# Last Z and Y staged whole in bf16, four PSUM tags from the third output unit, late units and output rows spread anew

## The chip, the cores and the metric

The kernel runs on one core of one Trainium2 chip. The metric is device time in microseconds (us), the median of several executions. A profile of one execution gives what each engine did: TensorE (PE, with PEld for its weight loads), VectorE (DVE), ScalarE (ACT), GpSimd (POOL) and SyncE (SP, which issues output DMAs here).

## The reference

Two layers follow each other. The first is a linear attention with feature maps; its result, with heads put side by side, is the input of the second, a mixing of the lowest 64 Fourier modes along the sequence, with a residual and a dense layer.

```python
batch, n_heads, seq, head_dim = (8, 8, 576, 64); d_feat = 128; d_model = 512; n_modes = 64
def phi(x):
    proj = np.einsum('bhsd,df->bhsf', x, w_phi)
    proj = proj - np.max(np.abs(proj), axis=-1, keepdims=True)
    return np.concatenate([np.exp(proj), np.exp(-proj)], axis=-1)
q_p, k_p = (phi(q), phi(k))
kv = np.einsum('bhsf,bhsd->bhfd', k_p, v)
num = np.einsum('bhsf,bhfd->bhsd', q_p, kv)
den = np.einsum('bhsf,bhf->bhs', q_p, np.sum(k_p, axis=2))[..., None] + 1e-06
x = (num / den).transpose(0, 2, 1, 3).reshape(B, S, H * D)

X = np.fft.rfft(x, axis=1)[:, :n_modes]            # Xr, Xi
Yr = einsum('bmd,mde->bme', Xr, w_r) - einsum('bmd,mde->bme', Xi, w_i)
Yi = einsum('bmd,mde->bme', Xr, w_i) + einsum('bmd,mde->bme', Xi, w_r)
y = np.fft.irfft(Yr + 1j * Yi, n=S, axis=1)        # other modes are zero
u = x + y
out = (u + np.maximum(u @ w_ch, 0.0)).astype(np.float32)   # (8, 576, 512)
```

## The kernel before, in words

A sequence of 576 positions is five chunks, c = 0 to 4: chunks 0 to 3 hold 128 positions each, chunk 4 holds 64. The attention runs over 32 steps, and its result stays in SBUF as `xs_all`, in bf16, one slot of 128 partitions x 512 per (batch b, chunk c), at index 5b + c. Beside it, the forward transform (`x_mm`) fills `XT`, and the mode products begin: 32 groups of weights (`weights`, DMAs on GpSimd's queue, three buffers) are multiplied in `mode_mm` and summed in `mode_sum`. The first 22 groups lie inside the attention's steps, the last ten in a loop behind it. GpSimd scales v in the attention (`vscale`, L270 and L275), VectorE divides (L335, L336).

`u @ w_ch` is split. x @ w_ch is made early, chunk by chunk, as `xw` (`flip_x`, `times_w`). The rest is the inverse transform of Y @ w_ch, called Z. So every output chunk is, with `CI` the inverse transform's matrix:

- psB = xw + CI * Z, then relu (ScalarE, L780) into the output tile;
- psA = x + CI * Y, then added to the output tile (VectorE, L793).

**Z and Y by batch.** The last eight groups of weights (gi = 0 to 7) give complete rows of Y; a pair of them, P = gi // 2, gives 32 rows (modes and parts) for all 8 batches. `by_batch` (L691) multiplies them by w_ch into `psZ` (PSUM tag T0) and by the identity into `psR` (tag T1). Both have 128 partitions: batch j + 4h lies in partitions 32j to 32j + 31, half h. The tiles `zall` and `yall`, which the inverse transform reads, want those rows in partitions 32P to 32P + 31 for each batch. So `copy` moves a quarter, 32 partitions x 2 x 512, at a time: Z by ScalarE (L712), Y by VectorE (L713). These calls are put in the list `copies` and taken from it one by one between other work. For the last pair, P = 3, there are five calls: the first half of Z and Y and batch 0; the second half and batch 4; then batches 1 and 5, 2 and 6, 3 and 7. One is made before the first output unit and one behind each of the units 0 to 3.

**Output units.** There are 20 units n: 16 whole units of two chunks (128 x 2 x 512), and four half units that pair chunk 4 of batches b and b + 4 (units 4, 9, 14 and 15). Units 0 to 4 are batches 0 and 4, 5 to 9 batches 1 and 5, 10 to 14 batches 2 and 6, 15 to 19 batches 3 and 7. For each, in this order of issue: `add_xw` (L771), `add_z` (L778 and the relu L780), `spec` (L787 x, L790 Y, and the add L793). psB and psA of a unit take PSUM tags T2 and T3, or T0 and T1:

```python
u["tags"] = ("T2", "T3") if n % 2 == 0 or n < 4 else ("T0", "T1")
```

A PSUM tag has one buffer, so a unit's first matmul into psA waits until VectorE's add has read the unit before it in that tag, and psB waits for the relu.

**Late units.** In ten whole units TensorE leaves x out of psA, and GpSimd adds it to the output tile afterwards (L797). For these, x is brought to output order earlier, by a permuting matmul and a ScalarE copy back into `xs_all` (`reordered`, L686 and L688), one or two at a time behind some groups of weights. `late` names them: units 2, 3, 5, 7, 8, 10, 12, 13, 16 and 17.

**Output DMAs.** SyncE issues them in program order, two per unit (256 KB each; 128 KB for a half unit): those of a late unit two units later (`LAG`), the others behind their own unit. Every engine works in program order; the order written here is kept as it is (`manual_schedule`).

Of the kernel before, what the change touches and what calls it, by code (L numbers as in the profile page):

```python
# [12 lines left out]
BF16 = mybir.dt.bfloat16  # L13
# [5 lines left out]
B_, H_, S_, D_ = 8, 8, 576, 64  # L19
NMODES = 64  # L20
DMODEL = 512
NCH = 5
# [4 lines left out]
def kernel(  # L27
# [11 lines left out]
    nc = tc.nc  # L39
# [116 lines left out]
    def weights(k):  # L156
        g, gi = groups[k]
        wt = {}
        for ri, w in ((0, moe_w_r), (1, moe_w_i)):
            t = pw.tile([128, 8, DMODEL], BF16, name=f"w{'ri'[ri]}", tag=f"w{ri}")  # L160
            if gi >= 0:
                nc.gpsimd.dma_start(  # L162
                    t, w[8 * gi:8 * gi + 8, g * 128:(g + 1) * 128, :].rearrange("m p e -> p m e"))
            else:
                for x in range(2):
                    mx = 16 * (-1 - gi) + 8 * x
                    nc.gpsimd.dma_start(
                        t[64 * x:64 * x + 64],
                        w[mx:mx + 8, g * 64:(g + 1) * 64, :].rearrange("m p e -> p m e"))
            wt[ri] = t  # L170
        W[k] = wt
# [252 lines left out]
    def mode_sum(k, psY, pb=None):  # L424
        g, gi = groups[k]
        if gi < 0:
            G = -1 - gi
            if g == 0:
                nc.vector.tensor_copy(Yacc[:, 2 * G:2 * G + 2, :], psY)
            else:  # L430
                nc.vector.tensor_tensor(
                    out=Yacc[:, 2 * G:2 * G + 2, :], in0=psY, in1=Yacc[:, 2 * G:2 * G + 2, :],
                    op=ALU.add)
        elif g < 3:
            nc.vector.tensor_tensor(  # L435
                out=Yacc[:, gi, :], in0=psY, in1=Yacc[:, gi, :], op=ALU.add)
        else:
            yst = pb.tile([128, DMODEL], BF16, name="yst", tag="yst", bufs=2)
            nc.vector.tensor_tensor(out=yst, in0=psY, in1=Yacc[:, gi, :], op=ALU.add)
            return yst  # L440
# [187 lines left out]
    pb = ctx.enter_context(tc.tile_pool(name="pb", bufs=2))  # L628
# [6 lines left out]
    yall = pb.tile([128, B_, DMODEL], BF16, name="yall", bufs=1)  # L635
    zall = pb.tile([128, B_, DMODEL], BF16, name="zall", bufs=1)
# [3 lines left out]
    todo = list(range(N_EARLY, B_ * NCH, 2))  # L640
    ahead = []
    copies = []
# [11 lines left out]
    def times_w():  # L654
        i, sT = ahead.pop(0)
        ps = psum.tile([128, 2, DMODEL], F32, name="psW", tag="T2")
        for x in range(2):
            for dc in range(4):
                nc.tensor.matmul(ps[:, x, :], lhsT=sT[:, x, dc, :], rhs=wchb[:, dc, :],  # L659
                                 start=(dc == 0), stop=(dc == 3))  # L660
        nc.scalar.copy(xw[:, i - N_EARLY:i + 2 - N_EARLY, :], ps)  # L661

    def pieces(n):
        for _ in range(n):
# [7 lines left out]
                copies.pop(0)()  # L672


    late = {0: ((1, 0), (1, 2)), 1: ((0, 0), (1, 0), (1, 2)), 2: ((0, 0), (1, 0), (1, 2)),
            3: ((0, 0), (0, 2))}
    reorder = sorted((b + 4 * x) * NCH + c for b in range(4) for x, c in late[b])

    def reordered(tag):
        i = reorder[0]  # L680
# [10 lines left out]
    def by_batch(sY, P):  # L691
        cols = [sY[:, dc].rearrange("p g c -> p (g c)") for dc in range(4)]
        psZ = psum.tile([128, 2, DMODEL], F32, name="psZ", tag="T0")
        psR = psum.tile([128, 2, DMODEL], F32, name="psR", tag="T1")

        def mm_z(h):
            for dc in range(4):
                for j in range(4):
                    nc.tensor.matmul(psZ[32 * j:32 * j + 32, h, :], lhsT=cols[dc][:, j + 4 * h::8],
                                     rhs=wchb[:, dc, :], start=(dc == 0), stop=(dc == 3))  # L700

        def mm_r(h):
            for dc in range(4):
                for j in range(4):
                    nc.tensor.matmul(
                        psR[32 * j:32 * j + 32, h, dc * 128:(dc + 1) * 128],
                        lhsT=cols[dc][:, j + 4 * h::8], rhs=ident_b, start=True, stop=True)

        def copy(j, h=None, one=False):
            r = slice(32 * j, 32 * j + 32)  # L710
            bs, hs = (slice(j, None, 4), slice(0, 2)) if h is None else (j + 4 * h, h)
            nc.scalar.copy(zall[32 * P:32 * P + 32, bs, :], psZ[r, hs, :])  # L712
            (nc.scalar.copy if one else nc.vector.tensor_copy)(  # L713
                yall[32 * P:32 * P + 32, bs, :], psR[r, hs, :])

        if P < 3:
            for f in (mm_z, mm_r):
                for h in range(2):
                    f(h)
            copies.extend([lambda j=j: copy(j) for j in range(4)])  # L720
        else:

            copies.extend([lambda: (mm_z(0), mm_r(0), copy(0, 0)),
                           lambda: (mm_z(1), mm_r(1), copy(0, 1)),
                           lambda: copy(1), lambda: copy(2), lambda: copy(3, None, True)])

    with tc.manual_schedule():
        plan = {22: 3, 23: 3, 24: 2, 25: 2, 26: 2, 27: 1, 28: 2, 29: 1, 30: 1, 31: 0}
        while k_out < 32:
            k = k_out  # L730
            gi = groups[k][1]
            while k_in < min(k_out + NW, 32):
                weights(k_in)
                k_in += 1
            yst = mode_sum(k, mode_mm(k, "T3"), pb)
            k_out += 1
            if yst is not None:
                if ahead:
                    times_w()
                pt = psum.tile([128, 4, 128], BF16, name="ptY", tag="T3")  # L740
                for dc in range(4):
                    nc.tensor.transpose(pt[:, dc, :], yst[:, dc * 128:(dc + 1) * 128], ident_b)
                if gi % 2 == 0:
                    sY = pb.tile([128, 4, 2, 128], BF16, name="sY", tag="sY")
                nc.vector.tensor_copy(sY[:, :, gi % 2, :], pt)
                if gi % 2 == 1:
                    by_batch(sY, gi // 2)
            pieces(plan[k])
            if k <= 24 or k % 2 == 0:
                assert not copies  # L750
                for tag in ("T0", "T1"):
                    if reorder:
                        reordered(tag)
            if k == 30:
                times_w()
        assert not todo and not ahead and not reorder and len(copies) == 5

# [39 lines left out]
    units = []  # L799
    for b in range(4):  # L800
        of = [pw.tile([128, 4, DMODEL], F32, name="of", tag=f"w{x}") for x in range(2)]
        o4 = Yacc[:, 2 * b, :]
        us = []
        for x in range(2):
            out_v = out[b + 4 * x].rearrange("(p n) e -> p n e", n=9)
            for c in (0, 2):
                us.append(dict(bc=((b + 4 * x, c), (b + 4 * x, c + 1)), o=of[x][:, c:c + 2, :],
                               late=(x, c) in late[b], half=False,
                               dmas=[(out_v[:, 5 * jj + c:5 * jj + c + 2, :],
                                      of[x][jj::2, c:c + 2, :]) for jj in range(2)]))  # L810
        u4 = dict(bc=((b, 4), (b + 4, 4)), o=o4, late=False, half=True,
                  dmas=[(out[b + 4 * x].rearrange("(p n) e -> p n e", n=9)[:, 4, :],
                         o4[64 * x:64 * x + 64]) for x in range(2)])
        units += [u4] + us if b == 3 else us + [u4]

    with tc.manual_schedule():
        LAG = 2
        copies.pop(0)()
        for n in range(len(units) + LAG):
            if n < len(units):  # L820
                u = units[n]
                u["tags"] = ("T2", "T3") if n % 2 == 0 or n < 4 else ("T0", "T1")
                add_xw(u)
                add_z(u)
                spec(u)
                if copies:
                    copies.pop(0)()
            for lag, is_late in ((LAG, True), (0, False)):
                if 0 <= n - lag < len(units) and units[n - lag]["late"] == is_late:
                    for dst, src in units[n - lag]["dmas"]:  # L830
                        nc.sync.dma_start(dst, src)

# [29 lines left out]
```

## Time and profile before

| what | us |
|---|---|
| median of 3 runs (460.96 to 462.92) | 460.98 |
| the profiled execution's own time | 459.81 |
| its span, first to last instruction | 458.02 |
| last weights land (wi of group 31) | 413.01 |
| last Z starts (L699) | 415.67 |
| last add on VectorE (L793) ends | 452.00 |
| last output DMA lands | 456.75 |
| busy in the span: PE / DVE / ACT / POOL | 302.9 / 299.2 / 263.7 / 195.2 |

Times in the views are counted from the start of the span. A row of a group gives its line, engine, operation, output and inputs with shapes, count, then busy time, the mean ns of one, and the idle time before them with what ended it. A row of a timeline gives start and duration. A row of the chain of waits gives the piece of work that the next piece waited for; "issue" is time in which nothing shown was waited for. The clock granted to TensorE is 1.00 of full speed in every stretch from 380 to 452.

### The profile page before, as it was taken

How to read it: one execution, taken by the hardware profiler on the slowest of the kernel's cores; microseconds unless marked ns; L12 is line 12 of the kernel's file. 1: busy time of each engine (PE TensorE's matmuls, PEld its weight loads, DVE VectorE, ACT ScalarE, POOL GpSimd, SP SyncE). 2: the span in 40 equal slices, each digit the busy share in tenths (PEclk: the TensorE clock that was granted, in tenths of full speed). 3: DMA queues.
4: the chain of work that ended last, by engine and by line, in shares of the span. 5: the costliest groups of instructions: out<-in, count | busy, mean ns of one | idle time of the engine just before them, and what ended most of it. 6: DMA issues, size and time to landing. Idle time of an engine off the chain costs nothing.

```text
span 458.0 us, 11074 instructions
## 1 busy us (share of the span) xinstructions
PE 302.9 (66%) x4637; PEld 196.9 (43%) x4637; DVE 299.2 (65%) x418; ACT 263.7 (58%) x531; POOL 195.2 (43%) x246
## 2 busy tenths in 40 slices
PE   3465687755587677646464665676678878867893
PEld 2354465543454545534343443343344544433341
DVE  6588889867988788866656473766332274464774
ACT  4575787843676868755545453755333445663762
POOL 4956567445563346634344332533021113000593
PEclk9987999975976979997769685988999999999998
DMA  6999999999999999999999999999999999991488
GB/s 181 193 230 216 213 210 218 229 207 229 218 218 218 229 218 229 219 228 217 219 207 221 216 219 218 207 209 206 207 207 207 207 207 207 207 173 50 170 317 292
DMA packets 84385, 97.31 MB, mean 212 GB/s; under 512 B 3312, under 2 KB 77168, under 8 KB 84336
## 3 DMA queue, kind: packets, MB, share of 16 engines
q0 software_dynamic: 75600, 76.49, 100.6%
q1 hardware_dynamic: 8576, 20.06, 12.6%
q8 instruction: 36, 0.59, 0.5%
q14 instruction: 13, 0.11, 0.1%
q10 hardware_dynamic: 160, 0.07, 0.1%
HBM read 163.64 MB, written 9.44 MB: 378 GB/s over the span
## 4 chain that ended last, share of the span: by engine, by line
DMA 30%; DVE 23%; issue 21%; PE 10%; POOL 7%; ACT 7%; SPq 1%; DVEq 0%; ACTq 0%; POOLq 0%
DMA wi<-in_moe_w_i_dram 19%; DVE mkq L233 7%; DMA wr<-in_moe_w_r_dram 7%; DMA q<-in_q_dram 4%; DVE xs_all L336 4%; DVE nd L322 3%; DVE tB L315 3%; ACT AA L240 3%; POOL vaug L270 2%; ACT e L262 2%; DVE of L793 2%; PE psNB L305 2%; PE psB L771 1%; PE psB L778 1%; PE psA L790 1%
## 5 line engine op out<-in xcount | busy, mean ns | idle before, releaser
L270 POOL TENSOR_TENSOR vaug<-vn,ee 128x576 bf16<-128x576 f32 x64 | 72.7, 1156 | 59.5 <-ACT ee L255 53.6
L240 ACT ACTIVATE AA<-psT 128x1024 bf16<-128x1024 f32 x64 | 62.0, 1021 | 42.3 <-PE psT L208 41.8
L162 POOL DMA_DIRECT2D wr<-in_moe_w_r_dram x24 | 21.9, 911 | 115.9 <-PE psY L416 109.5
L262 ACT ACTIVATE e<-mkq 64x4 f32<-64x4 f32 (+1 forms) x128 | 26.3, 206 | 66.3 <-DVE mkq L233 64.0
L244 ACT ACTIVATE AA<-psk 128x1024 bf16<-128x1024 f32 x64 | 61.3, 1009 | 0.0
L416 PE MATMUL psY<-wi,XT 128*32 128x512 bf16 x192 | 24.1, 448 | 29.1 <-DMA wi<-in_moe_w_i_dram 29.1
L416 PEld LDWEIGHTS <-XT 128*32 128x32 bf16 x384 | 17.7, 167 | 55.9 <-issue 47.9
L233 DVE TENSOR_REDUCE mkq<-psk 128x8 f32<-128x1024 f32 x32 | 38.8, 1212 | 0.8 <-PE psk L199 0.7
L233 DVE TENSOR_REDUCE mkq<-psq 128x8 f32<-128x1024 f32 x32 | 38.9, 1217 | 0.3
L435 DVE TENSOR_TENSOR Yacc<-psY,Yacc 128x512 f32<-128x512 f32 x16 | 11.0, 689 | 42.6 <-PE psY L416 42.5
L797 POOL TENSOR_TENSOR of<-of,xs_all 128x1024 f32<-128x1024 f32 x10 | 21.1, 2130 | 41.5 <-DVE of L793 41.5
L661 ACT CAST xw<-psW 128x1024 bf16<-128x1024 f32 x17 | 17.2, 1012 | 36.5 <-PE psW L659 36.5
L286 PE MATMUL kvz<-vaug,AA 64*128 64x65 bf16 x1152 | 29.5, 211 | 9.7 <-POOL vaug L275 8.0
L190 DVE COPY kT<-ptr 128x640 bf16<-128x640 bf16 x32 | 15.7, 491 | 30.5 <-PE ptr L184 30.5
L416 PE MATMUL psY<-wr,XT 128*32 128x512 bf16 x192 | 24.2, 458 | 16.0 <-DMA wr<-in_moe_w_r_dram 7.3
L315 DVE TENSOR_TENSOR tB<-psNB,e 128x650 f32<-128x650 f32 x32 | 26.6, 833 | 11.4 <-PE psNB L305 10.8
L659 PE MATMUL psW<-wchb,sT 128*128 128x512 bf16 x136 | 32.2, 379 | 2.1 <-ACT xw L661 2.1
L336 DVE TENSOR_TENSOR xs_all<-nd,rden 128x640 bf16<-128x640 f32 x32 | 31.6, 988 | 1.1
L305 PEld LDWEIGHTS <-AA 128*128 128x128 bf16 x640 | 28.4, 108 | 8.9 <-issue 8.5
L286 PEld LDWEIGHTS <-AA 64*128 64x128 bf16 x1152 | 25.3, 107 | 14.5 <-issue 10.4
L208 PE MATMUL psT<-qT,w 64*128 64x512 bf16 x64 | 14.6, 446 | 23.5 <-DVE mkq L233 23.3
L322 DVE TENSOR_TENSOR nd<-psNA,tB 128x650 f32<-128x650 f32 x32 | 26.7, 835 | 4.1 <-DVE tB L315 0.5
(130 smaller groups left out, 707.3 us busy)
## 6 DMA issues: line engine op xcount, KB each, us to landing
wr<-in_moe_w_r_dram POOLq DMA_DIRECT2D x24, 1024.0 KB, 24.3
wi<-in_moe_w_i_dram POOLq DMA_DIRECT2D x24, 1024.0 KB, 28.4
wr<-in_moe_w_r_dram POOLq DMA_DIRECT2D x16, 512.0 KB, 14.9
wi<-in_moe_w_i_dram POOLq DMA_DIRECT2D x16, 512.0 KB, 18.6
out_dram<-of SPq DMA_DIRECT2D x32, 256.0 KB, 2.4
vn<-in_v_dram SPq DMA_DIRECT2D x24, 288.0 KB, 5.7
q<-in_q_dram POOLq DMA_DIRECT2D x12, 288.0 KB, 19.5
k<-in_k_dram POOLq DMA_DIRECT2D x12, 288.0 KB, 19.3
```

The source lines that it names most:

```text
L233: nc.vector.tensor_reduce(out=o, in_=i, axis=AX.X, op=ALU.max, apply_absolute_value=True)
L240: nc.scalar.activation(AA[:, 0, ab, 0:1024].rearrange("f (x j p) -> f j x p", j=2, p=64), st["psT"].rearrange("f j (x p) -> f j x p", p=64 ...
L244: nc.scalar.activation(AA[:, 1, ab, 0:1024].rearrange("p (c j f) -> p j c f", c=4, j=2), st["psk"], ACT.Exp, scale=sc)
L262: nc.scalar.activation(e2[64 * jj:64 * jj + 64, hh, 0:NCH - jj], mkq[64 * hh:64 * hh + 64, 1, 5 * jj:5 + 4 * jj], ACT.Exp, scale=2.0)
L270: nc.gpsimd.tensor_tensor(out=vaug[:, ab, :, 0:64], in0=st["v"], in1=ee[:, ab, :].unsqueeze(2).to_broadcast([128, 9, D_]), op=ALU.mult,)
L286: nc.tensor.matmul(kvz[:, hh, ab * 65:(ab + 1) * 65], lhsT=AA[r, 1, ab, 128 * j:128 * j + 128], rhs=vaug[r, ab, j, :], start=(j == 0), sto ...
L305: nc.tensor.matmul(p[:, hh, 65 * c:65 * c + 65], lhsT=AA[:, 0, ab, x:x + 128], rhs=kvzF[:, hh, ab * 65:(ab + 1) * 65], start=True, stop=True,)
L315: nc.vector.tensor_tensor(out=tB, in0=st["psNB"], in1=e2.unsqueeze(3).to_broadcast([128, 2, NCH, 65]), op=ALU.mult,)
L322: nc.vector.tensor_tensor(out=nd, in0=st["psNA"], in1=st["tB"], op=ALU.add)
L336: nc.vector.tensor_tensor(out=xo, in0=nd[:, :, :, 0:64], in1=rden.to_broadcast([128, 2, NCH, 64]), op=ALU.mult,)
L416: nc.tensor.matmul(psY[32 * j:32 * j + 32, :], lhsT=XT[:, c0:c0 + 32, m], rhs=wt[ri][:, 2 * j + par, :], start=(par == 0 and ri == 0), sto ...
L659: nc.tensor.matmul(ps[:, x, :], lhsT=sT[:, x, dc, :], rhs=wchb[:, dc, :], start=(dc == 0), stop=(dc == 3))
```

## The change

For P = 3, each half of Z and Y is still made by TensorE as before, and batch 0's rows are copied from PSUM as before (`first`). Behind the second half (`rest`), ScalarE copies all of psZ, 128 x 1024, into a new bf16 tile `stz` in SBUF, and VectorE all of psR into `sty`. The rows of the other batches then move from these tiles into `zall` and `yall`, from SBUF to SBUF: batch 4 by VectorE at once (two copies of 32 x 512), batches 1 and 5 by GpSimd (two copies of 32 x 1024), batches 2 and 6 by VectorE behind unit 5, and 3 and 7 by VectorE behind unit 8 (two copies of 32 x 1024 each). ScalarE has no further copies.

Tags T0 and T1 are used from unit 3 on, and all four alternate from there.

Ten units are late as before, with unit 18 in place of unit 17. The order in which x is brought to output order is that of the index, so index 35 follows where 17 stood in between; behind weight group 24 there is one such copy instead of two, and behind group 30 two instead of one.

For batches 1, 2, 5 and 6 (units 5 to 8 and 10 to 13) the rows of chunks 0 to 3 go out together, in two DMAs of 512 KB per batch, behind the second of the two units (one unit later, or three where it is late). Other late units' DMAs come three units later instead of two. 32 output DMAs replace 40.

```diff
@@ -672,9 +672,8 @@
                 copies.pop(0)()
 
 
-    late = {0: ((1, 0), (1, 2)), 1: ((0, 0), (1, 0), (1, 2)), 2: ((0, 0), (1, 0), (1, 2)),
-            3: ((0, 0), (0, 2))}
-    reorder = sorted((b + 4 * x) * NCH + c for b in range(4) for x, c in late[b])
+    late = {(b, 0) for b in range(1, B_)} | {(4, 2), (5, 2), (6, 2)}
+    reorder = sorted(b * NCH + c for b, c in late)
 
     def reordered(tag):
         i = reorder[0]
@@ -706,23 +705,46 @@
                         psR[32 * j:32 * j + 32, h, dc * 128:(dc + 1) * 128],
                         lhsT=cols[dc][:, j + 4 * h::8], rhs=ident_b, start=True, stop=True)
 
-        def copy(j, h=None, one=False):
+        rows = slice(32 * P, 32 * P + 32)
+
+        def copy(j):
             r = slice(32 * j, 32 * j + 32)
-            bs, hs = (slice(j, None, 4), slice(0, 2)) if h is None else (j + 4 * h, h)
-            nc.scalar.copy(zall[32 * P:32 * P + 32, bs, :], psZ[r, hs, :])
-            (nc.scalar.copy if one else nc.vector.tensor_copy)(
-                yall[32 * P:32 * P + 32, bs, :], psR[r, hs, :])
+            nc.scalar.copy(zall[rows, j::4, :], psZ[r])
+            nc.vector.tensor_copy(yall[rows, j::4, :], psR[r])
 
         if P < 3:
             for f in (mm_z, mm_r):
                 for h in range(2):
                     f(h)
             copies.extend([lambda j=j: copy(j) for j in range(4)])
-        else:
-
-            copies.extend([lambda: (mm_z(0), mm_r(0), copy(0, 0)),
-                           lambda: (mm_z(1), mm_r(1), copy(0, 1)),
-                           lambda: copy(1), lambda: copy(2), lambda: copy(3, None, True)])
+            return
+
+
+
+        st = {}
+
+        def first():
+            mm_z(0)
+            mm_r(0)
+            nc.scalar.copy(zall[rows, 0, :], psZ[0:32, 0, :])
+            nc.vector.tensor_copy(yall[rows, 0, :], psR[0:32, 0, :])
+
+        def rest():
+            mm_z(1)
+            mm_r(1)
+            for nm, ps, f in (("z", psZ, nc.scalar.copy), ("y", psR, nc.vector.tensor_copy)):
+                st[nm] = pb.tile([128, 2, DMODEL], BF16, name=f"st{nm}", bufs=1)
+                f(st[nm], ps)
+            nc.vector.tensor_copy(zall[rows, 4, :], st["z"][0:32, 1, :])
+            nc.vector.tensor_copy(yall[rows, 4, :], st["y"][0:32, 1, :])
+            move(1, nc.gpsimd)
+
+        def move(j, eng):
+            r = slice(32 * j, 32 * j + 32)
+            eng.tensor_copy(zall[rows, j::4, :], st["z"][r])
+            eng.tensor_copy(yall[rows, j::4, :], st["y"][r])
+
+        copies.extend([first, rest, lambda: move(2, nc.vector), lambda: move(3, nc.vector)])
 
     with tc.manual_schedule():
         plan = {22: 3, 23: 3, 24: 2, 25: 2, 26: 2, 27: 1, 28: 2, 29: 1, 30: 1, 31: 0}
@@ -753,7 +775,7 @@
                         reordered(tag)
             if k == 30:
                 times_w()
-        assert not todo and not ahead and not reorder and len(copies) == 5
+        assert not todo and not ahead and not reorder and len(copies) == 4
 
 
 
@@ -801,32 +823,35 @@
         of = [pw.tile([128, 4, DMODEL], F32, name="of", tag=f"w{x}") for x in range(2)]
         o4 = Yacc[:, 2 * b, :]
         us = []
+        whole = b in (1, 2)
         for x in range(2):
             out_v = out[b + 4 * x].rearrange("(p n) e -> p n e", n=9)
             for c in (0, 2):
+                c0 = 0 if whole else c
+                is_late = (b + 4 * x, c) in late
                 us.append(dict(bc=((b + 4 * x, c), (b + 4 * x, c + 1)), o=of[x][:, c:c + 2, :],
-                               late=(x, c) in late[b], half=False,
-                               dmas=[(out_v[:, 5 * jj + c:5 * jj + c + 2, :],
-                                      of[x][jj::2, c:c + 2, :]) for jj in range(2)]))
-        u4 = dict(bc=((b, 4), (b + 4, 4)), o=o4, late=False, half=True,
+                               late=is_late, half=False, lag=3 if is_late else 1 if whole else 0,
+                               dmas=[(out_v[:, 5 * jj + c0:5 * jj + c + 2, :],
+                                      of[x][jj::2, c0:c + 2, :]) for jj in range(2)]
+                               if c == 2 or not whole else []))
+        u4 = dict(bc=((b, 4), (b + 4, 4)), o=o4, late=False, half=True, lag=0,
                   dmas=[(out[b + 4 * x].rearrange("(p n) e -> p n e", n=9)[:, 4, :],
                          o4[64 * x:64 * x + 64]) for x in range(2)])
         units += [u4] + us if b == 3 else us + [u4]
 
     with tc.manual_schedule():
-        LAG = 2
         copies.pop(0)()
-        for n in range(len(units) + LAG):
+        for n in range(len(units) + 3):
             if n < len(units):
                 u = units[n]
-                u["tags"] = ("T2", "T3") if n % 2 == 0 or n < 4 else ("T0", "T1")
+                u["tags"] = ("T2", "T3") if n % 2 == 0 or n < 2 else ("T0", "T1")
                 add_xw(u)
                 add_z(u)
                 spec(u)
-                if copies:
+                if n in (0, 5, 8):
                     copies.pop(0)()
-            for lag, is_late in ((LAG, True), (0, False)):
-                if 0 <= n - lag < len(units) and units[n - lag]["late"] == is_late:
+            for lag in (3, 1, 0):
+                if 0 <= n - lag < len(units) and units[n - lag]["lag"] == lag:
                     for dst, src in units[n - lag]["dmas"]:
                         nc.sync.dma_start(dst, src)
 
```

## The prediction

> **What bounds the kernel now.** I read the busy time by stretches first, for where each engine stands at the end of the run; then the chain of waits behind that stretch; then the groups by form, for durations; then the timeline of two places much earlier, where VectorE and GpSimd meet. The windows view (columns: PE, PEld, DVE, ACT, POOL busy, granted clock, DMA share, GB/s):
>
> ```profile
> core 0: us, PE busy (x) PEld busy (x) DVE busy (x) ACT busy (x) POOL busy (x), PEclk, DMA share, GB/s
> ...
> 413.00:417.00 4.00, 2.63 (x49) 1.69 (x49) 1.12 (x2) 0.18 (x1) 0.00 (x0) 1.00 0.02 4
> ...
> 421.00:429.00 8.00, 5.26 (x25) 1.80 (x23) 6.18 (x6) 7.57 (x8) 2.58 (x2) 1.00 0.33 132
> 429.00:437.00 8.00, 7.91 (x41) 3.33 (x40) 5.85 (x6) 4.67 (x6) 5.27 (x3) 1.00 0.74 270
> ```
>
> Until 413 the weights' DMA sets the pace. From 421 to 429 ScalarE is full (7.57 of 8 us) and TensorE is not; from 429 on TensorE is (7.91). The chain of waits says the same:
>
> ```profile
> 388.44 24.57 DMA wi<-in_moe_w_i_dram
> ...
> 422.21 1.24 DVE of L793
> ...
> 424.13 0.56 DVE yall L713
> 424.69 0.03 issue
> 424.72 1.24 DVE of L793
> ```
>
> The last weight lands at 413.01; nothing in the change makes it land sooner. In 421 to 428 the chain goes through VectorE's adds (L793) and the copies of Y between them (L713): units 0 to 4 share one PSUM pair (T2, T3), and each waits for the one before.
>
> ```profile
> L797 POOL TENSOR_TENSOR of<-of,xs_all 128x1024 f32<-128x1024 f32 x10 | 21.1, 2130 | 41.5 <-DVE of L793 41.5
> L793 DVE TENSOR_TENSOR of<-psA,of 128x1024 f32<-128x1024 f32 x16 | 19.6, 1224 | 7.9 <-ACT of L780 7.4
> ...
> L712 ACT CAST zall<-psZ 32x1024 bf16<-32x1024 f32 x3 | 3.0, 1002 | 0.1
> ...
> L713 DVE CAST yall<-psR 32x1024 bf16<-32x1024 f32 x2 | 2.4, 1222 | 0.1
> ```
>
> A copy of 32 rows out of PSUM costs ScalarE 1.00 and VectorE 1.22 us, as much as one of 128 rows (L661, 1.01 for 128x1024). That is what staging whole saves. The price is on another row: the new copies are VectorE copies from SBUF to SBUF in bf16 while GpSimd works. The kernel before has one such copy (L507):
>
> ```profile
> 107.33 2.43 DVE L507 COPY ident_p<-ident_b 128x128 bf16<-128x128 bf16 x1
> 107.39 2.27 POOL L270 TENSOR_TENSOR vaug<-vn,ee 128x576 bf16<-128x576 f32 x2
> ```
>
> A 128-column copy took 2.43 us and ended 0.10 us after two GpSimd operations did. Casts of 576 columns that met no GpSimd operation (L154) took 0.40 and 0.45. The same again with an operation of two SBUF inputs:
>
> ```profile
> 118.65 2.29 POOL L270 TENSOR_TENSOR vaug<-vn,ee 128x576 bf16<-128x576 f32 x2
> 118.66 0.22 DVE L335 RECIPROCAL rden<-nd 128x10 f32<-128x10 f32 x1
> 118.91 2.72 DVE L336 TENSOR_TENSOR xs_all<-nd,rden 128x640 bf16<-128x640 f32 x1
> ```
>
> L336 has a median of 825 ns; here 2.72, as at 33.63 (3.29). GpSimd's second operation went ahead of the waiting VectorE each time, three times with L507.
>
> **Part by part.** I laid the rows end to end from 415.67, where the last Z starts, engine by engine in program order: 0.43 us for a pair of 512-column matmuls (0.215 in a half unit), the relu 0.63 after the Z matmuls start, 1.02 for the relu (0.60), 1.23 for the add (0.68), 2.12 for GpSimd's add, 0.64 for each output DMA's issue, 2.37 from issue to landing, 1.3 from the last landing to the end of the span. The order of before gives a last add at 451.89 and a span of 457.98, measured 452.00 and 458.02. So the rules hold to 0.1 us, and differences below are against 457.98. That execution took 459.81 against a median of 460.98, 0.25% apart; I add the difference to the median.
>
> *Spread of late units.* Index 35 takes the place of 17, so the reordering copies of x shift: two instead of one after weight group 30. The second waits for the copies of Y that end at 410.51; then 0.43, a psW of 1.72, and the first four of group 31's matmuls can start at 412.8. The wi landing at 413.01 hides that with 0.04 us left; a late arrival would cost up to 0.3. I take 0.
>
> *Copies.* ScalarE loses four copies of 1.00 and two of 0.57 and gets 0.57 and 1.01: 5.14 to 1.58, 3.56 less. VectorE loses 2 x 0.68 and 2 x 1.22 = 3.80. It gets 0.68, one 1.22 (sty), two copies of 32x512 and four of 32x1024 between SBUF tiles. No row shows these. By bytes read, a 1024-column bf16 copy (2,048 B) is nearest the cast of 576 f32 columns (2,304 B, 0.40), and a 512-column one lies between L491 (512 B, 0.22) and that: 0.27. Upper ends are the PSUM copies in bf16, 0.69 (L651) and 0.42 (L745). I take 0.40 and 0.27: 4.04, so 0.24 more. GpSimd gets two copies (batches 1 and 5). Its cast of 576 columns takes 0.66 and one of 18 takes 0.25, so 1.00 for 1024; ends 0.66 and 1.3. Unit 5 needs them at 428, they end at 423: hidden by 5 us.
>
> *Four tags.* Unit 3 takes T0 and T1, free at 421.6 once stz and sty are made, instead of waiting for unit 2's.
>
> *Output rows.* 32 DMAs replace 40. The 128 KB and 256 KB rows both need 0.54 and 0.60 us to issue, so I take 0.64 for 512 KB too; bounds 0.54 and 1.2. SP is in order: each whole batch waits for its slowest unit, and smaller ones stand behind it. The last eight remain 256 KB. Unit 18's rows now go last and wait for GpSimd's add (2.12) instead of unit 17's: within 0.4 us of before, counted in the sums.
>
> *Where the new copies wait.* VectorE is in order, so a held copy holds every add behind it; TensorE then waits for psA two units later. End of VectorE's add, us:
>
> | add of unit | before | no hold | forecast |
> |---|---|---|---|
> | 1 | 423.44 | 423.47 | 424.81 |
> | 5 | 432.43 | 429.57 | 430.91 |
> | 6 | 433.72 | 431.69 | 434.75 |
> | 9 | 437.34 | 435.78 | 441.82 |
> | 19 | 452.00 | 449.58 | 455.62 |
>
> With no hold the relief is 2.9 us at unit 5; 1.7 us of copies (four of 0.40 and gaps), two before unit 6 and two before unit 9, partly give it back, and 2.75 remain at the end. With holds: (1) sty ends at 421.6; GpSimd copies since 421.0 and has the second queued, until 422.98. zall of batch 4 waits till then: 1.3 us. (2) Behind unit 5's add (430.91), GpSimd is in unit 3's add until 430.99; unit 5's is only just queued, so I let the first copy in there and the second wait until 433.09: 1.8 us. (3) Behind unit 8's add (437.27) GpSimd is in unit 7's add, with unit 8's queued, to 440.28: 3.0 us, and units 11 on wait for VectorE. The holds sum to 6.1 us; laid down with the rest they move the last add by 455.62 - 449.58 = 6.04. -2.75 + 6.04 = +3.3 us (span 461.27). 460.98 + 3.3 = **464.3**.
>
> **Rivals.** *Not held.* The copies run in a way that needs nothing of GpSimd's, as the reciprocal L335 (0.22 us in the midst of L270). Then -2.75: 458.2; with copies at 0.69, 459.7. Against it: L507 is the same kind of copy. This one decides the sign: it needs copy rows near 0.4 us while L819 runs.
>
> *In at the first gap.* VectorE gets in when GpSimd's current operation ends and keeps its place for both copies: waits of 0.4, 0.1 and 0.9. Span 456.45, -1.5: 459.5. For it: L336 at 118.91 did get in ahead of the third operation, L275. Against: never ahead of the second L270, and L819 follows L819.
>
> *One operation per copy.* Each copy waits for the GpSimd operation that runs, and the two engines take turns. Span 460.54, +2.6: 463.5. [...]
>
> *Mixed.* In at a gap at one or two of the places, held at the third: +0.2 to +1.7, about 461.6. The places differ by hundredths: unit 5's add above.
>
> *Nothing changes.* If PSUM freed earlier didn't matter, units 3 and 5 would stay at their times. The chain runs through T2 and T3 there, so I give this no chance.
>
> **How the numbers follow.** Held over GpSimd's run (forecast) 0.35, one per copy 0.22, not held 0.18, first gap 0.15, mixed 0.10. About 0.5% (2.3 us: 458.7 and 463.3) is what a measurement of this kernel can tell from no change. Faster: 0.15 of not held, 0.03 of first gap: 0.18. Slower: all the forecast's and 0.15 of one per copy: 0.50. The rest, 0.32, is within. Signs are mixed, so the range takes in not held at 458.0; above it ends with the forecast at the dearest copies (0.69, 0.42, GpSimd's 1.3): +5.06, 466.0. Outside remain some 0.12. The forecast's own range is 463.6 (GpSimd's copies at 0.66) to 466.0.
>
> **What would show it.** Right: the changed kernel's VectorE copies (L738, L739, L744, L745) of 2 us and more, ending just after an L819 or L745 on GpSimd; TensorE waiting for VectorE's add near units 8 and 11; unit 5's add near 431, a gain of 1.5 us, and unit 9's near 441. Wrong: these copies at 0.3 to 0.5 us while L819 runs, and a last add near 449.6. If ScalarE is still full from 421 to 429, or the wi landing is not at 413, the sum fails elsewhere.

## The result and the profile after

| | before | changed |
|---|---|---|
| median of 11 runs each, us | 461.29 | 466.05 |
| lowest and highest | 459.52, 463.57 | 463.99, 467.99 |
| span of the profiled execution | 458.02 | 466.21 |
| last weights land | 413.01 | 414.48 |
| last Z starts | 415.67 | 421.12 |
| from there to the end of the span | 42.35 | 45.09 |

The change makes the kernel slower: ratio 1.0092, interval 1.0068 to 1.0116, which is 4.2 us; the plain medians lie 4.8 apart. I forecast 3.3. The profiled execution of the changed kernel is the slowest of its 11 (467.99), so its 8.2 us over before are more than is typical. They fall into three: 1.47 because the weights land later (over the ten profiles of this document they land between 413.00 and 414.81); 3.98 between that landing and the last Z (6.64 against 2.66); and 2.74 behind the last Z.

The windows view of the changed kernel (columns as before):

```profile
413.00:417.00 4.00, 3.54 (x9) 1.17 (x8) 0.60 (x1) 2.02 (x2) 0.00 (x0) 0.50 0.10 17
...
421.00:429.00 8.00, 7.02 (x82) 3.74 (x85) 5.11 (x7) 3.89 (x5) 2.08 (x2) 1.00 0.18 69
...
437.00:445.00 8.00, 5.38 (x26) 2.03 (x26) 7.94 (x6) 4.33 (x5) 5.25 (x3) 1.00 0.64 257
```

ScalarE is relieved as laid down: from 421 to 429 it is busy 3.89 us where it was 7.57. The last Z starts 5.45 us later here, so these stretches don't cover the same work; in the 8 us that do (426.45 to 434.45) it is 4.11. But from 437 to 445 VectorE is full, 7.94 of 8 us in six instructions, and TensorE gets 5.38. And from 413 to 417, before any of the new copies, the granted clock is 0.50. These are two losses of their own.

**Behind the last Z.** VectorE's timeline, then GpSimd's:

```profile
426.96 0.78 DVE L738 COPY zall<-stz 32x512 bf16<-32x512 bf16 x1
427.66 1.13 DVE L739 COPY yall<-sty 32x512 bf16<-32x512 bf16 x1
...
436.29 0.42 DVE L744 COPY zall<-stz 32x1024 bf16<-32x1024 bf16 x1
436.63 2.35 DVE L745 COPY yall<-sty 32x1024 bf16<-32x1024 bf16 x1
...
442.52 1.34 DVE L744 COPY zall<-stz 32x1024 bf16<-32x1024 bf16 x1
443.78 2.34 DVE L745 COPY yall<-sty 32x1024 bf16<-32x1024 bf16 x1
```

```profile
426.56 1.03 POOL L744 COPY zall<-stz 32x1024 bf16<-32x1024 bf16 x1 [37.12 <-issue]
427.54 1.10 POOL L745 COPY yall<-sty 32x1024 bf16<-32x1024 bf16 x1
432.15 6.54 POOL L819 TENSOR_TENSOR of<-of,xs_all 128x1024 f32<-128x1024 f32 x3 [3.51 <-issue]
441.44 4.40 POOL L819 TENSOR_TENSOR of<-of,xs_all 128x1024 f32<-128x1024 f32 x2 [2.75 <-DVE of L815]
```

The same copy takes 0.42 or 2.35 us. The one at 436.29 came as unit 3's add on GpSimd ended (436.37) and went straight through; the next met unit 5's add and ended 0.29 us after it. The copy at 442.52 ended 0.29 us after unit 7's add (443.57), though unit 8's was already queued; the next waited for unit 8's and ended 0.29 us after it (445.84). So in this profile each held copy waited for the GpSimd operation that ran, and then the two engines took turns. GpSimd was held up too: its adds next to these copies (units 5 and 8) took 2.35 and 2.31 us, the others 2.12 to 2.14. The chain of waits shows whom the held copy holds up:

```profile
437.60 1.37 DVE yall L745
...
439.00 1.24 DVE of L815
...
440.28 0.59 PE psA L812 x2
```

TensorE (L812, unit 8) waits for unit 6's add, and that stands behind the held copy.

**Ahead of the last Z.** TensorE's timeline before, then in the changed kernel:

```profile
408.68 0.59 PE L686 MATMUL psX<-xs_all,ident_p 128*128 128x512 bf16 x2 [1.39 <-ACT zall L712]
409.11 1.89 PE L659 MATMUL psW<-wchb,sT 128*128 128x512 bf16 x8
```

```profile
412.18 1.01 PE L685 MATMUL psX<-xs_all,ident_p 128*128 128x512 bf16 x2 [1.78 <-ACT zall L712]
413.65 1.01 PE L685 MATMUL psX<-xs_all,ident_p 128*128 128x512 bf16 x2 [0.46 <-DVE yall L713]
414.46 3.62 PE L659 MATMUL psW<-wchb,sT 128*128 128x512 bf16 x8
```

The second x copy (psX) behind weight group 30 waits for Y's copies, and the eight psW matmuls behind it take 3.62 us, where before they took 1.89. With the weights there at 414.48, psY begins only at 418.01.

Two things mix here. The second x copy starts 1.47 us after the first, and psW stands behind it. And TensorE came late and slow to both: the weights of group 30 landed at 404.63 (before: 402.77), and the granted clock was 0.50 from 405.04 to 408.46 and again from 411.87 to 418.70. The second of these falls begins ahead of the first x copy (412.18), so in this profile it isn't the second one's doing.

### The profile page after: what moved, and what is told of

Read it like the earlier page. It is cut to its first block, busy times and chain, and to the rows that moved or that the text cites. A ratio compares the mean times of both kernels' runs of the same rounds, so it can differ in the third digit from the quotient of the medians.

```text
span 466.2 us, 11054 instructions
## 1 busy us (share of the span) xinstructions
PE 308.4 (66%) x4619; PEld 200.5 (43%) x4637; DVE 304.5 (65%) x422; ACT 260.8 (56%) x527; POOL 197.8 (42%) x248
## 5 line engine op out<-in xcount | busy, mean ns | idle before, releaser
L270 POOL TENSOR_TENSOR vaug<-vn,ee 128x576 bf16<-128x576 f32 x64 | 72.6, 1151 | 60.2 <-ACT ee L255 54.3
L659 PE MATMUL psW<-wchb,sT 128*128 128x512 bf16 x127 | 34.5, 405 | 2.7 <-ACT xw L661 2.1
L336 DVE TENSOR_TENSOR xs_all<-nd,rden 128x640 bf16<-128x640 f32 x32 | 30.7, 959 | 1.1
L184 PE MATMUL ptr<-ident_b,k 128*128 128x128 bf16 x160 | 18.3, 261 | 14.2 <-DVE qT L190 12.3
```

Of the source, the lines that this page charges most:

```text
L270: nc.gpsimd.tensor_tensor(out=vaug[:, ab, :, 0:64], in0=st["v"], in1=ee[:, ab, :].unsqueeze(2).to_broadcast([128, 9, D_]), op=ALU.mult,)
L336: nc.vector.tensor_tensor(out=xo, in0=nd[:, :, :, 0:64], in1=rden.to_broadcast([128, 2, NCH, 64]), op=ALU.mult,)
```

## The experiments

Three theories went in. A: the second x copy lets TensorE idle, its granted clock falls, and psW takes twice as long. B: VectorE's SBUF-to-SBUF copies are held by GpSimd. C, from the trace after: held by one operation each, in turns. Medians stand beside those of before on the same chip.

**e1: the late units of before in the changed kernel.**

```diff
-    late = {(b, 0) for b in range(1, B_)} | {(4, 2), (5, 2), (6, 2)}
+    late = {(4, 0), (4, 2), (1, 0), (5, 0), (5, 2), (2, 0), (6, 0), (6, 2), (3, 0), (3, 2)}
```

> The changed kernel with the late units of before (unit 17 late, not 18), so the x copies to output order stand as before: two behind weight group 24, one behind group 30. In the profile of the changed kernel the last Z starts at 421.12 (before: 415.67), and from there to the end it takes 45.09 us (before: 42.35). Theory A: the second x copy behind group 30 waits for Y's copies, TensorE idles and its granted clock falls to 0.50 from 411.87 to 418.70; that is about 2 us of the 4.8 in the medians. Then this kernel is about 2 us below the changed one (464.0 to 464.9, since unit 17's rows go last, up to 0.8), its clock stays at 1.00 from 405 to 415 in the profile, and its last Z starts near 416. Rival: the fall of the clock is chance and not bound to the late units. Then 466 to 467, and the clock falls here in some executions as well.

Measured: 465.24 against 461.33, ratio 1.0110 (1.0080 to 1.0141); not to be told from the changed kernel. In its profile the last Z starts 2.66 us after the weights land (416.50 and 413.83), as in before, so the loss ahead of Z is gone there. Behind Z it took 46.00 us, 0.91 more than the changed kernel, as unit 17's rows then go last (by hand up to 0.8); the clock was at 0.50 from 436.89 to 440.30. VectorE's last add ends 39.56 us after the last Z in both kernels, so the slow clock cost nothing by then and the 0.91 lies in the last output DMAs. Theory A wanted 2 us and a median of at most 464.9; with four runs the median alone doesn't settle it.

**e2: the late units of the change in the kernel before.**

```diff
-            3: ((0, 0), (0, 2))}
+            3: ((0, 0), (1, 0))}
```

> The kernel before with only the late units of the change (unit 18 late in place of 17), so the second x copy behind weight group 30. Theory A: about 2 us slower than before (463.3), with the last Z starting later than 415.7 and a granted clock below 1.00 in 405 to 419. Rival (chance): within 0.5 us of before, 461.3. My prediction took 0, at most 0.3, for this part.

Measured: 462.77 against 461.33, ratio 1.0035 (1.0010 to 1.0060). So this part alone costs 1.4 to 1.6 us. TensorE's timeline:

```profile
410.26 0.59 PE L686 MATMUL psX<-xs_all,ident_p 128*128 128x512 bf16 x2 [0.88 <-DVE yall L713]
410.69 3.36 PE L659 MATMUL psW<-wchb,sT 128*128 128x512 bf16 x8
```

The weights landed at 413.00, as in the profile of before, yet the last Z starts 1.28 us later, at 416.95: psW took 3.36 us, with a clock of 0.50 from 410.95 to 414.37. Here the wait for the second x copy does lie ahead of the fall. From Z on it took 42.24 us, as before.

**e3: VectorE's six SBUF-to-SBUF copies on ScalarE.**

```diff
-            nc.vector.tensor_copy(zall[rows, 4, :], st["z"][0:32, 1, :])
-            nc.vector.tensor_copy(yall[rows, 4, :], st["y"][0:32, 1, :])
+            nc.scalar.copy(zall[rows, 4, :], st["z"][0:32, 1, :])
+            nc.scalar.copy(yall[rows, 4, :], st["y"][0:32, 1, :])
...
-        copies.extend([first, rest, lambda: move(2, nc.vector), lambda: move(3, nc.vector)])
+        copies.extend([first, rest, lambda: move(2, nc.scalar.copy), lambda: move(3, nc.scalar.copy)])
```

> The changed kernel with VectorE's six SBUF-to-SBUF copies (batch 4, batches 2 and 6, 3 and 7) on ScalarE instead; all else as in the change. Theory B: these copies on VectorE are held by GpSimd's operations, 6 us in sum. On ScalarE nothing holds them: 1.0 us for 1024 columns and 0.57 for 512. Laid down by hand the span from the last Z on falls by 3.7 us against the changed kernel: 462.3, and VectorE's adds follow each other without a gap behind units 5 and 8. Rival: moving 32 partitions between SBUF tiles is slow on any engine (the PSUM copies of 32 rows cost as much as of 128). Then ScalarE's copies take 2 us too, and the time stays at 466 or goes up.

Measured: 461.74 against 461.33, ratio 1.0016 (0.9989 to 1.0043). ScalarE's timeline, while GpSimd adds:

```profile
432.51 1.04 ACT L744 COPY zall<-stz 32x1024 bf16<-32x1024 bf16 x1
433.46 1.04 ACT L745 COPY yall<-sty 32x1024 bf16<-32x1024 bf16 x1
```

Nothing held them: 1.04 us each. From the last Z to the end it took 41.78 us, and 45.09 in the changed kernel; by hand 41.9 (the forecast's 45.6 less 3.7). The copies' engine is worth more than 3 us.

The loss ahead of Z is still in (4.10 us from landing to Z), and this time not by a slow psW. TensorE's timeline:

```profile
412.20 0.59 PE L685 MATMUL psX<-xs_all,ident_p 128*128 128x512 bf16 x2 [1.79 <-ACT zall L712]
413.67 0.59 PE L685 MATMUL psX<-xs_all,ident_p 128*128 128x512 bf16 x2 [0.88 <-DVE yall L713]
414.10 1.89 PE L659 MATMUL psW<-wchb,sT 128*128 128x512 bf16 x8
```

The clock is 1.00 here; it had been 0.50 from 404.67 to 408.08, behind weights of group 30 that landed at 404.79. TensorE reaches the x copies 3.5 us later than before, and then the 1.47 us between the two copies is no longer hidden by the last weights (414.66).

**e4: GpSimd idle in the last stage.**

```diff
-    late = {(b, 0) for b in range(1, B_)} | {(4, 2), (5, 2), (6, 2)}
+    late = set()
...
-            move(1, nc.gpsimd)
+            move(1, nc.scalar)
...
+            (nc.scalar.copy if eng is nc.scalar else eng.tensor_copy)(zall[rows, j::4, :], st["z"][r])
+            (nc.scalar.copy if eng is nc.scalar else eng.tensor_copy)(yall[rows, j::4, :], st["y"][r])
```

> The changed kernel with nothing for GpSimd in the last stage: no late units (TensorE adds x in all 20) and the copies of batches 1 and 5 on ScalarE; VectorE's six copies stay where they are. The reordering copies of x fall away too. Theory B: VectorE's copies of 1024 columns take 0.40 and those of 512 take 0.27 (ends 0.69 and 0.42), none near 2 us. TensorE gets ten more pairs of matmuls, 4.3 us. By hand a span of 456.9, 1.0 below before: about 460.2. Rival: the copies are slow in themselves; then rows of 1 to 2.4 us remain.

Measured: 462.98 against 461.33, ratio 1.0049 (1.0029 to 1.0070), 2.8 us over what I laid down. For theory B the rows count, VectorE's timeline:

```profile
423.88 0.29 DVE L738 COPY zall<-stz 32x512 bf16<-32x512 bf16 x1
424.09 0.28 DVE L739 COPY yall<-sty 32x512 bf16<-32x512 bf16 x1
...
434.78 0.42 DVE L744 COPY zall<-stz 32x1024 bf16<-32x1024 bf16 x1
435.12 0.41 DVE L745 COPY yall<-sty 32x1024 bf16<-32x1024 bf16 x1
```

With GpSimd idle no copy exceeds 0.42, so the copies are not slow in themselves: B is shown. The time missed by about what two things come to. My sum forgot that the copies of batches 1 and 5, moved to ScalarE, stand ahead of unit 1's relu (2.08 us). And here the clock was at 0.50 from 412.65 to 419.48, behind a wait of 2.93 us for weights and without any x copy, with the last Z 3.50 us after the landing instead of 2.66: in this profile the clock fell behind other idle time.

**e5: the second x copy behind psW.**

```diff
                     if reorder:
                         reordered(tag)
-            if k == 30:
-                times_w()
+                    if k == 30 and tag == "T0":
+                        times_w()
```

> The changed kernel with one order altered: behind weight group 30 TensorE does the first x copy, then the eight psW matmuls, then the second x copy, so it no longer idles for Y's copies ahead of psW. Theory A (the idle time lets the granted clock fall to 0.50, and psW then takes twice as long): as late units alone cost 1.4 us over before, this kernel is 1.4 to 2 us below the changed one, 464.0 to 464.6, with the last Z starting within 3.0 us of the last weights' landing (before: 2.66; changed: 6.64). Rival: the second x copy costs its own 0.43 us and a wait wherever it stands, or the clock falls by chance; then 465.5 to 466.5.

Measured: 463.08 against 460.89, ratio 1.0054 (1.0027 to 1.0082), where the changed kernel has 1.0092. TensorE's timeline:

```profile
412.30 0.59 PE L685 MATMUL psX<-xs_all,ident_p 128*128 128x512 bf16 x2 [1.79 <-ACT zall L712]
412.73 1.89 PE L659 MATMUL psW<-wchb,sT 128*128 128x512 bf16 x8
414.46 0.59 PE L685 MATMUL psX<-xs_all,ident_p 128*128 128x512 bf16 x2
```

psW is back at 1.89 and the last Z starts, at 417.82, 3.00 us after the weights (414.81). Behind Z it took 45.10, as in the changed kernel. So the order of one x copy is worth 1.0092 - 1.0054 = 0.38%, 1.8 us by the point values (the intervals overlap), which agrees with e2. The 0.54% that is left, 2.5 us, is near the 2.74 us that the profiles show behind Z.

Ten profiles side by side say what the order does. With the order of before (before, e1) the last Z starts 2.66 us after the weights; with that of e5 (e5 to e7) 2.66 to 3.00; with that of the change 6.64 (changed), 3.95 (e2), 4.10 (e3) and 3.99 (e8). In e3 and e8 psW took 1.89, as before. So the order costs 1 us and more in each, but theory A is only one way to that cost: a clock of 0.50 at psW in two of the four, the second copy's wait itself, met late, in the other two.

**e6: e5, and the copies ahead of GpSimd's first late unit.**

```diff
-            move(1, nc.gpsimd)
...
-        copies.extend([first, rest, lambda: move(2, nc.vector), lambda: move(3, nc.vector)])
+        copies.extend([first, rest, lambda: (move(1, nc.scalar.copy), move(2, nc.vector.tensor_copy),
+                                             move(3, nc.vector.tensor_copy))])
...
-                if n in (0, 5, 8):
+                if n in (0, 1):
```

> The kernel of e5, and the copies of batches 2, 6, 3 and 7 on VectorE directly behind unit 1, before GpSimd has any late unit; the copies of batches 1 and 5 on ScalarE there. Theory C: held copies are the whole loss behind the last Z, and VectorE's copies of 1024 columns take 0.42. By hand a span of 455.7 on before's landing of the weights: 2.3 below before, 459.0. Rival: the early copies only move the loss (unit 2 starts 1.7 us later, and TensorE runs out of work earlier on); then 461 to 462.

Measured: 457.25 against 460.89, ratio 0.9918 (0.9886 to 0.9950): faster than both, and 1.75 us below what I laid down. VectorE's timeline, then GpSimd's:

```profile
424.94 0.42 DVE L743 COPY zall<-stz 32x1024 bf16<-32x1024 bf16 x1
...
426.05 0.42 DVE L744 COPY yall<-sty 32x1024 bf16<-32x1024 bf16 x1
```

```profile
428.06 4.22 POOL L819 TENSOR_TENSOR of<-of,xs_all 128x1024 f32<-128x1024 f32 x2 [36.31 <-DVE of L815]
```

All four are through before GpSimd starts. From the last Z to the end it took 39.90 us (by hand 40.0) against 42.35 before. The 2.45 us are what staging and four tags, with the new late units and output rows, are worth when nothing holds the copies; the parts weren't taken one by one, but for the rows (e7).

**e7: e6 with the output rows of before.**

```diff
-        whole = b in (1, 2)
+        whole = False
...
-                               late=is_late, half=False, lag=3 if is_late else 1 if whole else 0,
+                               late=is_late, half=False, lag=2 if is_late else 1 if whole else 0,
...
-            for lag in (3, 1, 0):
+            for lag in (2, 0):
```

> The kernel of e6 with the output DMAs of before: two of 256 KB per whole unit, late units two units later, 40 in all. Theory: the rows of whole batches are hidden but for the last eight, which are alike: within 0.5 us of e6 (459.0). Rival: 32 issues instead of 40 free SyncE and matter near the end; then e7 is 1 us or more above e6.

Measured: 458.50 against 460.89, ratio 0.9950 (0.9923 to 0.9976). From the last Z on 40.27 us against 39.90 in e6: 0.4, as the theory has it. The medians lie 1.25 apart, as the rival has it, but the intervals overlap; whether the rows are worth anything stays open.

**e8: Z and Y in one tile, one copy per move.**

```diff
+    zyall = pb.tile([128, 2, B_, DMODEL], BF16, name="zyall", bufs=1)
+    zall, yall = zyall[:, 0], zyall[:, 1]
...
-            eng.tensor_copy(zall[rows, j::4, :], st["z"][r])
-            eng.tensor_copy(yall[rows, j::4, :], st["y"][r])
+            eng.tensor_copy(zyall[rows, :, j::4, :], st["zy"][r])
```

> The changed kernel with Z and Y side by side in one tile, staged and final, so each move is one copy of 2048 columns instead of two of 1024 (batch 4: one of 1024). Late units, output rows and the place of the moves are those of the change. Theory C (each VectorE copy waits for the GpSimd operation that runs, then the two engines take turns): the second copies' waits, 0.85, 1.93 and 1.92 us in the changed kernel's profile, fall away; copies of 0.85 us plus at most one wait of a GpSimd operation each. By hand 4.0 us less: 462.0. Rival (my forecast's: a copy waits until GpSimd has no more work queued): the move behind unit 8 waits over two GpSimd operations, 3 us and more, and the time falls by 2 us or less: 464 or more.

Measured: 460.02 against 460.89, ratio 0.9968 (0.9940 to 0.9996), 2 us below what I laid down. VectorE's timeline, then GpSimd's:

```profile
431.50 0.81 DVE L743 COPY zyall<-stzy 32x2048 bf16<-32x2048 bf16 x1
...
435.96 1.49 DVE L743 COPY zyall<-stzy 32x2048 bf16<-32x2048 bf16 x1
```

```profile
434.77 6.76 POOL L817 TENSOR_TENSOR of<-of,xs_all 128x1024 f32<-128x1024 f32 x3 [0.47 <-DVE of L813]
```

The move behind unit 8 waited 0.7 us, for unit 7's add, and went ahead of unit 8's, in the midst of GpSimd's three adds in a row. That is theory C; by my forecast's rule it would have waited 3 us and more. From Z on it took 40.05 us. The same work in the same places, with half the copies, saves 5 us behind Z where I had 4.0 by hand: the loss is in the number of turns. Part of it is arrival: GpSimd's one copy now waits for `stzy` whole, so VectorE's copy for batch 4 came 0.07 us ahead of it (423.39 and 423.46) and met nothing, and the move behind unit 5 came as unit 3's add ended (431.75).

## Why the prediction was right, and where it was not

The sign and its reason held: the copies on VectorE meet GpSimd's adds (e4: 0.42 without them, 2.35 with), and that outweighs the relief of ScalarE (e3, e6). The predicted copies "of 2 us and more" are in the trace, two of the six; so are "unit 5's add near 431", counted from the last Z (15.24 us after it forecast, 15.14 measured), and "TensorE waiting for VectorE's add near units 8 and 11". The median of 466.05 lies at the upper end of the range, 466.0; the ratio on the 460.98 that the forecast started from gives 465.2.

The prices fit: copies 0.42 and 0.28 (taken 0.40 and 0.27), GpSimd's copy 1.03 (1.00), the issue of a 512 KB DMA 0.47 to 0.60 (0.64, with its gap). The working of before's last stage carried over: with the rule of turns it gives 2.6 us over before, against 2.74 in the profile.

*The rule of the hold* failed as I put it: GpSimd's queued operation did not go ahead of VectorE here. The rival "one operation per copy" is what happened in this stage: the copy at 442.52 ended 0.29 us after unit 7's add, with unit 8's queued. That the price hardly differs is luck: over the free copies the six rows are 0.5, 0.85, 0, 1.9, 0.9 and 1.9 us longer, 6.1 in sum, and my three places gave 6.1. At each place stand two copies, and at the last GpSimd had just two adds to do, so two turns of one operation cost what I had put down as one wait over two. e8, with one copy per place, is where the two rules part. Why L336 and L507 waited over two operations in the attention is open; it was not tried. A third L336 there, at 247.21, came while the second L270 ran and waited for that one alone (1.57 us).

*The spread of late units* was mis-sized: I took 0, at most 0.3 for a late arrival, and it costs 1.4 to 1.8 us by the medians (e2, e5). The term failed in two ways. It priced psW at 1.72 us whatever TensorE did before, and with a clock of 0.50 it took 3.36 (e2) and 3.62 (changed). And it took a late arrival for the last weights alone; when those of group 30 came late too, TensorE reached the x copies 3.5 us later, and with psW at 1.89 the last Z still started 1.44 us later behind the landing than before (e3). Which of the two an execution meets, the medians don't tell. With this term the sum comes to 4.1 to 4.5 (2.74 and 1.4 to 1.8), against 4.2 by the ratio and 4.8 by the plain medians.

## What to carry to other kernels

VectorE's copies between SBUF tiles took 0.28 to 0.42 us while GpSimd was still (e4) and up to 2.35 beside its adds (changed): put such copies where GpSimd has nothing, or make few long ones instead of many short, since two of the four copies of 1024 columns waited 1.9 us, most of a GpSimd add of 2.13 (changed). Before giving a step a price of 0 because a wait hides it, look at what runs behind the wait, and at what happens to the wait when the work ahead of it comes late: here TensorE's clock fell from 1.00 to 0.50 behind idle time, and psW then took 3.36 (e2) and 3.62 us (changed) instead of 1.89. A last stage laid down row by row against the profile of before came within 0.1 to 0.2 us in e3, e6 and, with the rule of turns, the changed kernel; it missed by 1 us in e8 and by 3 in e4, and such misses point at what the sum left out.

## What the runs showed of the hardware

In the profiles of before and changed the granted clock is 1.00 or 0.50, and every record of it but the last is a whole multiple of 3.41 us long. In ten profiles (before, changed, e1 to e8) I set TensorE's matmul busy time in each step of 3.41 us that ends between 300 and 452 us, while matmuls still run, against the clock of the next. The clock fell from 1.00 to 0.50 in 25 places; in 22 of them matmuls were busy 46% of the step or less, and in the other three 48 to 53%. Only three steps under 46% were not followed by a fall, and no step over 55% was followed by one, of some 350; in between it went either way. None of the four falls in before and changed had a step without matmuls ahead of it: the step before was busy 39% (ending at 318.30 in before), 33, 42 and 48% (405.04, 411.87 and 319.71 in changed). In the profile of before the step at 410.46 was busy 52% and the clock stayed at 1.00.

ScalarE copied 1024 columns of bf16 from SBUF to SBUF in 1.04 us, about as long as from PSUM (1.00), and was not held by GpSimd (the same 1.04 in e3 beside GpSimd's adds and in e4 without them). VectorE's copy and GpSimd's add held each other up: the copy of 0.42 us took 2.35 (changed), and GpSimd's add of 2.13 us took 2.35 beside a copy of 1024 columns (changed) and 2.58 beside one of 2048 (e8).
